# The second MLP's second product by Strassen's algorithm, with its weight forms built during attention

## The chip, the cores and the metric

The kernel runs on one core of a Trainium2 chip. The metric is the device time of one execution in microseconds (us); three timed runs of the kernel before gave a median of 886.11 us.

## The reference

Attention with a block-causal mask (4 batches, 8 heads, 576 positions, head dimension 64), then two MLPs over the 2304 tokens of width 512:

```
scores = q @ k.T / 8, masked where block(i) < block(j) (blocks of 64); softmax; attn @ v
x  = heads side by side                                  # 2304 x 512
x  = max(x @ w1, x @ w2, x @ w3) @ w_out                 # first MLP, hidden width 768
h  = max(x @ w_in, 0)                                    # second MLP, hidden width 2048
out = (h * h) @ w_out                                    # 2304 x 512
```

Weights of the MLPs come in double precision, read as pairs of 32-bit words; everything else is float32.

## The kernel before

**Precision.** A product of two float32 matrices is made of three TensorE products in float32r: each operand is split into a high part (a copy that rounds) and a low part (the subtraction of that copy), and low x high, high x low and high x high are summed in PSUM. So each product costs three matmuls per 128 x 128 block of weights, and each operand costs one copy (mostly on ScalarE) and one subtraction (on VectorE). `load_w_` (line 381) turns a block of 128 x 512 double-precision weights into float32 with integer operations: two ScalarE instructions, two on VectorE, one integer addition on GpSimd.

**Order of work.** All instructions go through a planner (`Plan`, line 187 issues them; so nearly every row of the profile has line 187). It knows an estimated length and a rank for each, and places them by a list schedule: on each engine the one that can start first, and among those the lowest rank, then program order. The result is one fixed order per engine and one for the DMA queue on SyncE (SP). There are two such plans, ended by `nc.issue()`: the first has attention, the first MLP up to its fifth of eight parts, and the preparation of w_out; the second has the rest of the first MLP, the preparation of w_in, and the second MLP. `nc.behind(marks[WO][0])` (line 781) holds back the preparation of w_out until the exponential of a certain attention step has been made; steps are counted in program order (20 steps for the first batch, 20 for each later one).

**Attention and first MLP.** Four batches, four head pairs each; `mlp1(b, g)` works on 256 or 320 tokens of a batch with the weights stationary. Its matmuls (tile `l` in the profile) fill TensorE beside attention, and what is left of them runs alone before the second MLP. Its output y goes to DRAM transposed (features by tokens).

**Second MLP, first product (up).** Three passes over 768 tokens each. In a pass the tokens form two halves of 384 columns, and features and hidden rows are cut in two as well, so that Strassen's algorithm (in Winograd's form) takes seven products p1 to p7 in place of eight. Its weight forms (a11, a12, a22 and four sums s1 to s4) are made once per block q (of eight): `second_rows` and `first_rows` (lines 806 and 810) load two row blocks, sum them on GpSimd and split them into `wq` [128, 7, 2, 256], which goes to DRAM as one piece of 1.79 MB and comes back in one piece per block and pass. Four blocks fit in the chip at a time, and the first pass uses the last four as they are made. `up(p, q)` (line 894) makes the seven products, 6 matmuls of 384 columns for each, with two PSUM banks X and Y; `part` and `finish` combine them on VectorE and ScalarE, apply relu and square, and split the result g.

**Second MLP, second product (down).** `down(p, q)` (line 946) is the plain product: for the four quarters of a block (two row blocks, two token halves) and three groups of 128 tokens, g is stationary and w_out moving, 3 matmuls of 512 columns each: 36 per block, summed over all eight blocks of a pass in six PSUM banks `acc`. It runs one block behind `up` and interleaved with it. w_out was split into high and low parts during late attention (tile `wos`, rows of `wo_d`); each block loads them again in pieces of 256 KB (tiles `wol`, `woh`). The output is tokens by features.

Of the kernel before, what the change touches and what calls it, by code (L numbers as in the profile page):

```python
# [44 lines left out]
CFG = dict(PD=-1, PE=1, A1=0, A2=0, WP=1, FC=(8, 16), WO=55, FI=0, LO2=0, HI2=0, Q2=0, RN=3, XL=2, HL=2, SO=0, TF=0, W_A=0.7, W_B=1.5, SPARE='hl..rhl..rhl..r..r..r', S=15, PB=3, QB=(2, 2, 3), BANKS=(3, 2, 1, 2), LO=0, HI=0, Q=0, EV=('*', '*'), EV2=('a', 'a'), CB=2, PC=0, PM=1000, PX=-0.5, PO=0, HH='*', XH='*', N0='a', YS='a', HIS=0, RB=1, TB=(2, 1), KB=1, CT='a', LT='d', XA=4, XB=0)  # L45
# [302 lines left out]
def fused_kernel(ctx: ExitStack, tc: tile.TileContext, z0, k0, qk, v, w123, wo1, win2, wo2, out):  # L348
# [15 lines left out]
    wo_d = dram.tile([NC2, 128, 2, DM], F32, name="wo_d")  # L364
    wq_d = dram.tile([NQ, 128, 7, 2, 256], F32, name="wq_d")
# [15 lines left out]
    def load_w_(src, hi, lo, name, f=None):  # L381
        spare = SPARE[len(chunks)] if len(chunks) < len(SPARE) else "."
        chunks.append(name)
        if spare in "hl":
# [9 lines left out]
        nc.sync.dma_start(out=raw, in_=src.bitcast(U32).rearrange("p (n t) -> p n t", t=2))  # L394
# [15 lines left out]
        if hi is None:  # L410
            return
# [26 lines left out]
    def load_wo1(c):  # L438
        wo1_t[c] = [m1.tile([128, DM], F32R, tag=f"wo1{x}{c}", name=f"wo1{x}{c}") for x in "hl"]
        load_w(wo1[128 * c:128 * c + 128, :], *wo1_t[c], f"wo1_{c}")  # L440
# [70 lines left out]
    def new_x(b, g):  # L511
        if (b, g) not in x_t:
            w = GROUPS[g][1]
            x_t[b, g] = [m1.tile([128, KC, w], F32R, tag=f"{t}{g}", name=f"{t}{b}_{g}") for t in ("xh", "xl")]
        return x_t[b, g]
# [264 lines left out]

    with nc.behind(marks[CFG["WO"]][0]), nc.ranked(2):
# [17 lines left out]
    wq_t, forms_f = {}, {}  # L799
    WB = 4  # L800

    def wq_tile(q):
        wq_t[q] = w2p.tile([128, 7, 2, 256], F32R, tag="wq", bufs=WB, name=f"wq{q}")
        return wq_t[q]

    def second_rows(q):
        f = forms_f[q] = w2p.tile([128, 8, 256], F32, tag="wqf", name=f"wqf{q}")
        load_w_(win2[q + NQ], None, None, f"wi_{q + NQ}", f[:, 0:2].rearrange("p i n -> p (i n)"))

    def first_rows(q):  # L810
        f, w = forms_f[q], wq_tile(q)
        load_w_(win2[q], None, None, f"wi_{q}", f[:, 2:4].rearrange("p i n -> p (i n)"))
        a21, a22, a11, a12, s1, s2, s3, s4 = [f[:, i] for i in range(8)]
# [3 lines left out]
        for i, j in ((0, 3), (3, 7)):  # L817
            nc.scalar.copy(out=w[:, i:j, 0], in_=f[:, i + 1:j + 1])
            nc.vector.tensor_tensor(out=w[:, i:j, 1], in0=f[:, i + 1:j + 1], in1=w[:, i:j, 0].bitcast(F32), op=ALU.subtract)
        nc.sync.dma_start(out=wq_d[q], in_=w.bitcast(F32))  # L820
# [16 lines left out]
    PRODUCTS = dict(p1=(1, "b11"), p2=(2, "b21"), p6=(4, "t2"), p5=(3, "t1"), p7=(5, "t3"), p3=(6, "b22"), p4=(0, "t4"))  # L837
# [27 lines left out]
    wo_t, g_t = {}, {}  # L865
    G_HOMES = [(m1, "xh0"), (m1, "xl0"), (m1, "xh1"), (m1, "xl1"), (m1, "hh"), (m1, "hl"), (w1p, "w1l5")]
    C_HOMES = ["wo1h4", "wo1l4", "wo1h5", "wo1l5"]
    homes = [0, 0]

    def wo_tiles(p, m):  # L870
        i = 2 * (m % NQ % 2) + m // NQ
        wo_t[p, m] = [m1.tile([128, DM], F32R, tag=f"wo1{c}{i}", name=f"wo{c}{p}_{m}") for c in "hl"]
        return wo_t[p, m]

    def load_wo(p, m):
        for c, t in enumerate(wo_tiles(p, m)):
            nc.sync.dma_start(out=t.bitcast(F32), in_=wo_d[m, :, c])

    def g_tiles(name):
        pool, tag = G_HOMES[homes[0] % len(G_HOMES)]  # L880
        homes[0] += 1
        g = pool.tile([128, 2, TH], F32R, tag=tag, name=name)
        return g[:, 0], g[:, 1]

    def split_g(key, c):
        gh, gl = g_t[key] = g_tiles("g%d_%d_%d_%d" % key)
        nc.scalar.copy(out=gh, in_=c)
        nc.vector.tensor_tensor(out=gl, in0=c, in1=gh.bitcast(F32), op=ALU.subtract)

    def c_tile(name):  # L890
        homes[1] += 1
        return m1.tile([128, TH], F32, tag=C_HOMES[homes[1] % len(C_HOMES)], name=name)

    def up(p, q):

        w, x = wq_t[q], x_s[p]
        X, Y = [bank(f"ph{p}_{q}_{b}", "mlp")[:, :TH] for b in "xy"]

        def product(acc, name):
            i, form = PRODUCTS[name]  # L900
            hi, lo = x[form]
            for k in range(2):
                ws = slice(128 * k, 128 * k + 128)
                for c, (s, r) in enumerate(((1, hi), (0, lo), (0, hi))):
                    mm(acc, w[:, i, s, ws], r[:, k], start=k == 0 and c == 0, stop=k == 1 and c == 2)
            if q == NQ - 1 and p + 1 < NPASS:
                split_tokens(p + 1, form)

        def part(acc, name, other=None):
            t = m1.tile([128, TH], F32, tag="xf", bufs=4, name=f"{name}_{p}_{q}")  # L910
            if other is None:
                nc.scalar.copy(out=t, in_=acc)
            else:
                nc.vector.tensor_tensor(out=t, in0=acc, in1=other, op=ALU.add)
            return t

        def finish(m, h, acc, other):
            c = c_tile(f"c{p}_{q}_{m}{h}")
            nc.vector.tensor_tensor(out=c, in0=acc, in1=other, op=ALU.add)
            nc.vector.scalar_tensor_tensor(out=c, in0=c, scalar=0.0, in1=c, op0=ALU.max, op1=ALU.mult)  # L920
            split_g((p, q, m, h), c)

        product(X, "p1")
        p1 = part(X, "p1")
        product(Y, "p2")
        finish(0, 0, Y, p1)
        yield 3
        product(X, "p6")
        u2 = part(X, "u2", p1)
        product(Y, "p5")  # L930
        u4 = part(Y, "u4", u2)
        yield 2
        product(X, "p7")
        finish(1, 1, X, u4)
        u3 = part(X, "u3", u2)
        yield 2
        product(Y, "p3")
        finish(0, 1, Y, u4)
# [43 lines left out]
    with nc.ranked(1):  # L982
        before = iter(())
        stream = [(p, q) for p in range(NPASS) for q in range(NQ)]
        for j, (p, q) in enumerate(stream):
# [13 lines left out]
            for _ in before:  # L999
                pass  # L1000
# [48 lines left out]
```

## Time and profile before

| | us |
|---|---|
| timed runs, median (lowest to highest) of 3 | 886.11 (885.11 to 886.7) |
| the profiled execution, span from first to last instruction | 886.9 |
| TensorE busy in it | 864.2 |
| VectorE, ScalarE, GpSimd busy | 601.1, 424.9, 104.0 |
| first matmul of the second MLP starts at | 501.71 |
| last matmul of all starts at | 881.76 |

The span is that of one execution with the profiler on; the timed runs are others. Busy time of TensorE is modelled from the starts of its matmuls and their lengths, and the matmuls overlap; the pace of a stretch is read from the starts, not from the busy time of one.

### The profile page before, as it was taken

The page shows a single profiled execution, that of the slowest core. Times are in us where ns is not written, and L with a number is a line of the kernel's source. Part 1 is how long each engine was busy: PE and PEld are TensorE (multiplying, and loading weights), DVE is VectorE, ACT ScalarE, POOL GpSimd, SP SyncE. Part 2 cuts the span into 40 slices and gives each one's busy share as a digit, 9 for nine tenths or more (in the row PEclk, how much of TensorE's full clock was granted, in tenths as well). Part 3 has the DMA queues.
Part 4 walks back from the last instruction along what each step waited for, and adds up shares of the span by engine and source line. Part 5 has one row for each costly group of instructions (what it writes and reads, how often), then busy time and mean ns, then how long its engine had stood idle before and what let it go on. Part 6 is the DMA issues. An engine that isn't in the chain of part 4 may idle for free.

```text
span 886.9 us, 14852 instructions
## 1 busy us (share of the span) xinstructions
PE 864.2 (97%) x5464; PEld 777.7 (88%) x5464; DVE 601.1 (68%) x1376; ACT 424.9 (48%) x1016; POOL 104.0 (12%) x94
## 2 busy tenths in 40 slices
PE   5899999999999999999999989999999999999997
PEld 4567799998999989899999979898999989999896
DVE  6998678878788988646557766546755457544543
ACT  6888667667688787544555231113211114211111
POOL 2233200000001111214442230000000000000000
PEclk9999999999999999999999999999999999999999
DMA  8745432232255563554656578454765536655221
GB/s 294 237 138 174 131 114 89 85 115 86 85 184 177 175 213 118 196 190 165 257 203 237 164 299 338 160 230 168 270 229 184 207 145 229 215 200 196 72 72 71
DMA packets 52056, 157.73 MB, mean 178 GB/s; under 512 B 8592, under 2 KB 16016, under 8 KB 48400
## 3 DMA queue, kind: packets, MB, share of 16 engines
q1 hardware_dynamic: 51984, 156.78, 50.5%
q8 instruction: 43, 0.70, 0.3%
q14 instruction: 29, 0.24, 0.1%
HBM read 124.26 MB, written 32.51 MB: 177 GB/s over the span
## 4 chain that ended last, share of the span: by engine, by line
PE 92%; DVE 2%; DMA 2%; ACT 2%; issue 0%; POOL 0%; SPq 0%; ACTq 0%; POOLq 0%; DVEq 0%
PE l L187 34%; PE acc L187 22%; PE ph_x L187 11%; PE ph_y L187 8%; PE av L187 5%; PE sc L187 5%; PE tp L187 4%; PE sc_t L187 2%; DMA raw_wi<-in_win 1%; PE tp_t L187 1%; DMA raw_wo<-in_wo 1%; DMA zk<-in_k 1%; PE r L187 0%; ACT P L187 0%; DVE f_wo L187 0%
## 5 line engine op out<-in xcount | busy, mean ns | idle before, releaser
L187 PE MATMUL acc<-woh,g 128*128 128x512 f32 x576 | 198.5, 395 | 0.0
L187 PE MATMUL l<-xh,w1l 128*128 128x256 f32 (+1 forms) x576 | 174.3, 303 | 0.9 <-DVE run L187 0.9
L187 PE MATMUL l<-xl,w1h 128*128 128x256 f32 (+1 forms) x576 | 172.2, 299 | 0.0
L187 PE MATMUL l<-xh,w1h 128*128 128x256 f32 (+1 forms) x576 | 172.2, 299 | 0.0
L187 ACT CAST g<-c 128x384 fp32r<-128x384 f32 x96 | 49.3, 513 | 220.8 <-DVE c L187 220.8
L187 PEld LDWEIGHTS acc<-woh,g 128*128 128x128 f32 x576 | 108.5, 189 | 19.4
L187 PE MATMUL acc<-wol,g 128*128 128x512 f32 x288 | 113.3, 393 | 0.0
L187 PEld LDWEIGHTS l<-xh,w1l 128*128 128x128 f32 x576 | 109.0, 189 | 4.1 <-issue 1.5
L187 PEld LDWEIGHTS l<-xl,w1h 128*128 128x128 f32 x576 | 109.1, 189 | 2.6 <-issue 1.7
L187 PEld LDWEIGHTS l<-xh,w1h 128*128 128x128 f32 x576 | 109.1, 189 | 1.9 <-issue 1.2
L187 PE MATMUL ph_x<-t,wq 128*128 128x384 f32 x432 | 87.7, 337 | 2.7 <-ACT p L187 2.7
L187 PEld LDWEIGHTS ph_x<-t,wq 128*128 128x128 f32 x432 | 77.4, 188 | 8.9 <-ACT p L187 3.1
L187 DVE TENSOR_TENSOR g<-c,g 128x384 fp32r<-128x384 f32 x96 | 53.6, 560 | 43.0 <-ACT g L187 42.6
L187 ACT ACTIVATE P<-sc,nm 128x128 f32<-128x128 f32 (+3 forms) x128 | 66.9, 530 | 9.9 <-DVE nm L187 8.4
L187 DVE TENSOR_TENSOR run<-l,run 128x256 f32<-128x256 f32 (+1 forms) x96 | 43.7, 455 | 27.9 <-PE l L187 26.3
L187 POOL TENSOR_TENSOR f_wo<-f_wo,raw_wo 128x512 int32<-128x512 int32 x22 | 29.8, 1357 | 276.5 <-DVE sm L187 180.3
L187 PEld LDWEIGHTS acc<-wol,g 128*128 128x128 f32 x288 | 54.3, 189 | 7.8
L187 PE MATMUL l<-hh,wo1l 128*128 128x256 f32 (+1 forms) x192 | 57.7, 306 | 2.2 <-DVE wo1l L187 2.1
L187 PE MATMUL ph_y<-b,wq 128*128 128x384 f32 x288 | 58.3, 337 | 0.0
L187 PE MATMUL l<-hl,wo1h 128*128 128x256 f32 (+1 forms) x192 | 57.5, 301 | 0.0
L187 PE MATMUL l<-hh,wo1h 128*128 128x256 f32 (+1 forms) x192 | 57.4, 300 | 0.0
L187 DVE TENSOR_REDUCE nm<-sc 128x2 f32<-128x256 f32 (+2 forms) x96 | 55.1, 588 | 0.8
(135 smaller groups left out, 1613.1 us busy)
## 6 DMA issues: line engine op xcount, KB each, us to landing
wq<-wq_d SPq DMA_DIRECT2D x20, 1792.0 KB, 8.6
wq_d<-wq SPq DMA_DIRECT2D x8, 1792.0 KB, 7.7
raw<-in_qk SPq DMA_DIRECT2D x24, 576.0 KB, 3.8
wol<-wo_d SPq DMA_DIRECT2D x48, 256.0 KB, 3.2
woh<-wo_d SPq DMA_DIRECT2D x48, 256.0 KB, 4.8
raw_wo<-in_wo SPq DMA_DIRECT2D x22, 512.0 KB, 3.8
raw_w<-in_w SPq DMA_DIRECT2D x18, 512.0 KB, 5.0
wo_d<-wos SPq DMA_DIRECT2D x16, 512.0 KB, 3.1
```

The source lines that it names most:

```text
L187: return getattr(engine, op_name)(*map(value, args), **{k: value(x) for k, x in kw.items()})
```

## The change

The second product of the second MLP goes through the same seven products as the first. For that:

- the output is made transposed (features by tokens), w_out's forms are stationary and g is moving, 384 columns at a time; the program returns the transpose of what it wrote;
- `down_forms(q)` builds the seven forms of each of eight blocks of w_out (sums on GpSimd, one copy and one subtraction for each form of 256 columns) and stores each with a DMA of 256 KB. It starts at attention step 24 in place of 55;
- `up_forms(q)` builds the forms of w_in with rank 0.5 in place of 2, all eight blocks in order, with the raw rows loaded one block ahead, and stores all of them to DRAM;
- both products now work on pairs of blocks j (four per pass). A unit of weights is one form of one pair (512 KB, two DMAs); 56 units per pass pass through a ring of nine tiles, in which the raw rows and the staged forms of w_in had their place before;
- in both products partial sums stay in PSUM: p1 is copied out and p6 is added on top of it in the same bank, and so on. Four banks per pair in up, six per pass in down;
- a pass is now four up pairs, then all of down; sums and splits of g are made in place ahead of the products that need them.

```diff
-CFG = dict(..., WO=55, ...)
+CFG = dict(..., WO=24, ...)
...
+    def split_form(pool, tag, bufs, f, dest, name):
+        n = f.area.shape[1] // 256
+        both = pool.tile([128, n, 2, 256], F32R, tag=tag, bufs=bufs, name=name)
+        f = f.rearrange("p (i n) -> p i n", n=256)
+        nc.scalar.copy(out=both[:, :, 0], in_=f)
+        nc.vector.tensor_tensor(out=both[:, :, 1], in0=f, in1=both[:, :, 0].bitcast(F32), op=ALU.subtract)
+        nc.sync.dma_start(out=dest.rearrange("i p h n -> p i h n"), in_=both.bitcast(F32))
+    def down_forms(q):
+        f = [load_w_(wo2[128 * m:128 * m + 128, :], None, None, f"wo_{m}") for m in (q, q + NQ)]
+        a11, a21, a12, a22 = [x[:, 256 * i:256 * i + 256] for x in f for i in range(2)]
...
+        combine(s1, a21, a22, ALU.add)
+        split(a11, "a11")
+        combine(a21, a11, a21, ALU.subtract)
+        split(a22, "a22")
...
     with nc.behind(marks[CFG["WO"]][0]), nc.ranked(2):
-        for m in (m for q in range(NQ) for m in (q, q + NQ)):
-            t = at.tile([128, 2, DM], F32R, tag="wos", name=f"wos{m}")
-            load_w_(wo2[128 * m:128 * m + 128, :], t[:, 0], t[:, 1], f"wo_{m}")
-            nc.sync.dma_start(out=wo_d[m], in_=t.bitcast(F32))
+        for q in range(NQ):
+            down_forms(q)
...
+    def up_forms(q):
+        fa, fs = [w2p.tile([128, 4, 256], F32, tag="gq", bufs=5, name=f"w{x}{q}") for x in ("fa", "fs")]
+        if q == 0:
+            load_raw(0)
+        if q + 1 < NQ:
+            load_raw(q + 1)
...
+        for f, i, j in ((fa[:, 1:2], 0, 1), (fa[:, 2:4], 1, 3), (fs[:, 0:2], 3, 5), (fs[:, 2:4], 5, 7)):
+            split_form(w2p, "ws", RING, f.rearrange("p i n -> p (i n)"), ws_d[0][q][i:j], f"wst{q}_{i}")
-    with nc.ranked(2):
-        for q in (*range(WB, NQ), *range(WB)):
-            second_rows(q)
-            first_rows(q)
+    with nc.ranked(0.5):
+        for q in range(NQ):
+            up_forms(q)
...
+    UP = ("p1", "p2", "p6", "p5", "p7", "p3", "p4")
+    DOWN = ("p1", "p5", "p6", "p3", "p7", "p2", "p4")
...
+    for p in range(NPASS):
+        stream += [(0, j, WEIGHT[i]) for j in range(NPQ) for i in UP]
+        stream += [(1, j, WEIGHT[i]) for i in DOWN for j in range(NPQ)]
...
+            u = w2p.tile([128, 2, 2, 256], F32R, tag="ws", bufs=RING, name=f"ws{len(units)}")
+            for a in range(2):
+                nc.sync.dma_start(out=u[:, a].bitcast(F32), in_=ws_d[s][2 * j + a][FORMS[form]])
...
+    BANKS_UP = ((("mlp", "mlp"), ("tp", "tp")), (("sc", "sc"), ("sc", "av")))
+    BANKS_DOWN = ((("mlp", "mlp"), ("tp", "tp"), ("sc", "sc")), (("sc", "sc"), ("sc", "av"), ("tp", "tp")))
+    def up(p, j):
+        X, Y = banks(BANKS_UP[(p + j) % 2], f"ph{p}_{j}")
+        acc = dict(p1=X, p6=X, p7=X, p4=X, p2=Y, p5=Y, p3=Y)
...
+        for name in UP:
+            w = next_unit()
+            hi, lo = x_s[p][TOKENS[name]]
+            for a in range(2):
+                o = acc[name][a]
+                for k in range(2):
+                    ws = slice(128 * k, 128 * k + 128)
+                    for c, (s, r) in enumerate(((1, hi), (0, lo), (0, hi))):
+                        mm(o, w[:, a, s, ws], r[:, k], start=name in ("p1", "p2", "p5") and k == 0 and c == 0, ...)
+                if name in ("p1", "p6", "p5"):
+                    nc.scalar.copy(out=keep[name, a], in_=o)
...
+    def ahead(p, j):
+        first_g[p, j] = split_g(p, "p1", j, g_c[j, "b11"])
+        sum_g(j, "t1")
+        sum_g(j, "t3")
+    def down(p):
+        X, Z, Y = banks(BANKS_DOWN[p % 2], f"acc{p}")
+        acc = dict(p1=X, p6=X, p7=X, p4=X, p5=Z, p3=Z, p2=Y)
+        for name in DOWN:
+            for j in range(NPQ):
+                if name == "p1":
+                    hi, lo = first_g.pop((p, j))
+                else:
+                    if form in ("t2", "t4"):
+                        sum_g(j, form)
+                    hi, lo = split_g(p, name, j, g_c[j, HELD[form]])
+                w = next_unit()
+                for a in range(2):
+                    for n in range(2):
+                        ns = slice(128 * n, 128 * n + 128)
+                        for c, (s, r) in enumerate(((1, hi), (0, lo), (0, hi))):
+                            mm(acc[name][n], w[:, a, s, ns], r[:, a], ...)
...
+                up(p, j)
+                ahead(p, j)
+            down(p)
```

## Rows read from the trace of the kernel before

**Rows 1.** The page: span, and busy us (share) xinstructions of TensorE and VectorE.
```profile
span 886.9 us, 14852 instructions
...
PE 864.2 (97%) x5464; PEld 777.7 (88%) x5464; DVE 601.1 (68%) x1376; ACT 424.9 (48%) x1016; POOL 104.0 (12%) x94
```

**Rows 2.** Windows of 20 us: length, busy (count) by engine, PEclk, DMA share, GB/s.
```profile
260.00:280.00 20.00, 20.00 (x148) 17.94 (x147) 17.86 (x52) 17.84 (x48) 2.62 (x2) 1.00 0.49 169
...
500.00:520.00 20.00, 17.30 (x94) 15.88 (x93) 13.33 (x24) 8.28 (x15) 6.52 (x7) 1.00 0.91 338
520.00:540.00 20.00, 20.00 (x95) 18.15 (x94) 13.83 (x24) 4.79 (x9) 5.94 (x6) 0.91 0.71 264
```

**Rows 3.** TensorE's timeline at the second MLP's start: start, length, [idle before].
```profile
501.71 1.20 PE L187 MATMUL ph_x<-b,wq 128*128 128x384 f32 x6
...
506.93 0.39 PE L187 MATMUL acc<-woh,g 128*128 128x512 f32 x1
...
516.42 0.40 PE L187 MATMUL acc<-woh,g 128*128 128x512 f32 x1
519.52 1.50 PE L187 MATMUL ph_x<-t,wq 128*128 128x384 f32 x6 [2.70 <-ACT p L187]
...
524.67 0.39 PE L187 MATMUL acc<-woh,g 128*128 128x512 f32 x1
```

**Rows 4.** The chain of waits in order of time: start, length, what (xcount).
```profile
369.51 132.36 PE l L187 x972
...
507.94 10.06 DMA raw_wi<-in_win
...
688.06 2.08 PE acc L187 x9
...
735.08 2.08 PE acc L187 x9
```

**Rows 5.** ScalarE's timeline at the stall of 516 us.
```profile
516.67 0.65 ACT L187 ACTIVATE raw_wi<-raw_wi 128x512 int32<-128x512 uint32 x1 [4.05 <-DMA raw_wi<-in_win]
...
519.00 0.47 ACT L187 COPY p<-ph_x 128x384 f32<-128x384 f32 x1
```

**Rows 6.** Groups by form: operation, shapes, count, busy us, mean ns, idle before.
```profile
L187 DVE SCALAR_TENSOR_TENSOR c<-c 128x384 f32<-128x384 f32 x96 | 53.6, 560 | 2.0
...
L187 POOL TENSOR_TENSOR wqf<-wqf 128x256 f32<-128x256 f32 x32 | 26.9, 862 | 1.2
...
L187 DVE TENSOR_TENSOR wos<-f_wo,wos 128x512 fp32r<-128x512 f32 x16 | 12.1, 754 | 11.6 <-ACT wos L187 10.9 <-ACT run L187 0.6
...
L187 DVE TENSOR_TENSOR t<-t,t 128x768 fp32r<-128x768 f32 x12 | 11.3, 952 | 2.0 <-ACT t L187 2.0
L187 DVE TENSOR_TENSOR hl<-run,hh 128x256 fp32r<-128x256 f32 x24 | 11.1, 464 | 1.8 <-ACT hh L187 1.4
...
L187 ACT CAST wos<-f_wo 128x512 fp32r<-128x512 f32 x16 | 9.9, 620 | 10.7 <-DMA wo_d<-wos 10.7
...
L187 ACT CAST hh<-run 128x256 fp32r<-128x256 f32 x16 | 6.5, 406 | 8.3 <-DVE run L187 8.0
```

**Rows 7.** A window of 1 us within output-weight loads, columns as in rows 2.
```profile
825.00:826.00 1.00, 1.00 (x6) 0.83 (x5) 0.96 (x2) 0.00 (x0) 0.00 (x0) 1.00 0.99 336
```

**Rows 8.** DMA issues: count, KB each, median us from issue to landing.
```profile
wol<-wo_d SPq DMA_DIRECT2D x48, 256.0 KB, 3.2
```

**Rows 9.** Waits of SP's queue: us in total, times, longest.
```profile
SPq L187 <- DVE wos L187: 23.4, 9, 6.9
```

**Rows 10.** The tile wos: ns min/median/max, first and last start.
```profile
L187 DVE TENSOR_TENSOR wos<-f_wo,wos x16: 664/689/1851, 272.6 to 392.0; 128x512 fp32r<-128x512 f32 x16
```

**Rows 11.** Timelines at the end: TensorE's last row, VectorE's last row.
```profile
881.76 0.39 PE L187 MATMUL acc<-woh,g 128*128 128x512 f32 x1
...
882.59 1.05 DVE L187 COPY ob<-acc 128x256 f32<-128x256 f32 x2 [2.43 <-ACT ob L187]
```

More of the change, by code (lines that the diff above doesn't have):

```diff
@@ L393, in load_w_ @@
                 f = m1.tile([128, 512], F32, tag="wf", bufs=2, name=f"f_{name}")
-        nc.sync.dma_start(out=raw, in_=src.bitcast(U32).rearrange("p (n t) -> p n t", t=2))
+        if src is not None:
+            nc.sync.dma_start(out=raw, in_=src.bitcast(U32).rearrange("p (n t) -> p n t", t=2))
         low, high = raw[:, :, 0], raw[:, :, 1]
@@ L438, in load_wo1 @@
     def load_wo1(c):
-        wo1_t[c] = [m1.tile([128, DM], F32R, tag=f"wo1{x}{c}", name=f"wo1{x}{c}") for x in "hl"]
+        if not wo1_t:
+            both = m1.tile([128, NC1, 2, DM], F32R, tag="wo1", name="wo1")
+            wo1_t.update({i: [both[:, i, x] for x in range(2)] for i in range(NC1)})
         load_w(wo1[128 * c:128 * c + 128, :], *wo1_t[c], f"wo1_{c}")
@@ L513, in new_x @@
             w = GROUPS[g][1]
-            x_t[b, g] = [m1.tile([128, KC, w], F32R, tag=f"{t}{g}", name=f"{t}{b}_{g}") for t in ("xh", "xl")]
+            both = m1.tile([128, 2, KC, w], F32R, tag=f"xhl{g}", name=f"xhl{b}_{g}")
+            x_t[b, g] = [both[:, i] for i in range(2)]
         return x_t[b, g]
@@ L894, in up @@
[L894 to L910, printed above, removed]
+    NPQ = NQ // 2
@@ new lines, in next_unit, with make_homes @@
+    def next_unit():
+        while len(units) < used[0] + RING:
+            n = len(units)
+            load_unit()
+            if len(units) == n:
+                break
+        used[0] += 1
+        return units[used[0] - 1]
+    C_HOMES = [("xhl1", 3), ("hh", 2), ("hl", 2), ("wo1", 8), ("xhl0", 1)]
+    g_c = {}
+    def make_homes():
+        places = []
+        for tag, n in C_HOMES:
+            t = m1.tile([128, n, 2, TH], F32, tag=tag, name=f"c_{tag}")
+            places += [t[:, i] for i in range(n)]
+        for j in range(NPQ):
+            for f in ("b11", "b12", "b22", "b21"):
+                g_c[j, f] = places.pop(0)
@@ new lines, in fused_kernel, with split_g, temp @@
+    turn_g = [0]
+    def split_g(p, name, j, f):
+        home = turn_g[0] % 6
+        turn_g[0] += 1
+        both = (w2p.tile([128, 2, 2, TH], F32R, tag="gq", bufs=5, name=f"g{p}_{name}_{j}") if home else
+                w1p.tile([128, 2, 2, TH], F32R, tag="w1l5", name=f"g{p}_{name}_{j}"))
+        nc.scalar.copy(out=both[:, 0], in_=f)
+        nc.vector.tensor_tensor(out=both[:, 1], in0=f, in1=both[:, 0].bitcast(F32), op=ALU.subtract)
+        return both[:, 0], both[:, 1]
+    def temp(tag, bufs, name):
+        return m1.tile([128, TH], F32, tag=tag, bufs=bufs, name=name)
@@ new lines, in fused_kernel, with banks, finish @@
+    BANKS_UP = ((("mlp", "mlp"), ("tp", "tp")), (("sc", "sc"), ("sc", "av")))
+    BANKS_DOWN = ((("mlp", "mlp"), ("tp", "tp"), ("sc", "sc")), (("sc", "sc"), ("sc", "av"), ("tp", "tp")))
+    def banks(tags, name):
+        return [[bank(f"{name}_{x}{i}", t)[:, :TH] for i, t in enumerate(pair)] for x, pair in zip("xzy", tags)]
+    def up(p, j):
+        X, Y = banks(BANKS_UP[(p + j) % 2], f"ph{p}_{j}")
+        acc = dict(p1=X, p6=X, p7=X, p4=X, p2=Y, p5=Y, p3=Y)
+        keep = {}
+        def finish(a, form, f, other):
+            c = g_c[j, form][:, a]
@@ L911, in part @@
             if other is None:
-                nc.scalar.copy(out=t, in_=acc)
+                nc.scalar.copy(out=c, in_=f)
             else:
[L914 to L919, printed above, removed]
-            nc.vector.scalar_tensor_tensor(out=c, in0=c, scalar=0.0, in1=c, op0=ALU.max, op1=ALU.mult)
-            split_g((p, q, m, h), c)
@@ L923, in up @@
[L923 to L938, printed above, removed]
-        yield 2
-        product(X, "p4")
-        finish(1, 0, X, u3)
-        yield 3
```

193 lines of the change are left out of this document (96 added, 97 removed).

## The prediction

> **What bounds the kernel now.** I read the page first: TensorE is busy 97% of a span of 886.9 us, VectorE 68% [rows 1]. A busy share of 97% can hide slow stretches, so I went to the second MLP, the stage that the change rewrites. Windows of 20 us show its two edges: TensorE is full with the granted clock at 1.00 on either side, and in 500:520 and 520:540 it loses time and the clock falls to 0.91 [rows 2]. The timeline gives the price of one matmul there, from start to start. The stage starts at 501.71; its first five up products (30 matmuls of 384 columns, nothing between them) take until 506.93, so 5.22/30 = 0.174 us each [rows 3]. The chain of waits repeats a pattern, one block of FF rows (42 up, 36 down matmuls) per period; three periods lie between 688.06 and 735.08, so 15.673 us each [rows 4]. Up takes 42 x 0.174 = 7.31 of it, and 8.37/36 = 0.232 us is left for a down matmul of 512 columns. The chain in this stretch names TensorE alone: no wait ends last there. So work taken off TensorE in this stage comes off the end, one for one, until another engine or the DMA is late.
>
> The one stall of the stage is at its start. TensorE's next matmul after 516.42 starts at 519.52, 2.70 us idle, released by ScalarE's copy p [rows 3]. That copy starts at 519.00, behind a weight conversion for which ScalarE had sat idle 4.05 us until a DMA of raw w_in rows landed [rows 5]; the chain shows that DMA as the piece of 10.06 us from 507.94 on [rows 4]. The 18 matmuls from 519.52 to 524.67 then run at about half the pace, at the lower of the clock's two levels in part (0.91 over the 20 us) [rows 2, 3]: 5.15 us for 12 x 0.174 + 6 x 0.232 = 3.48. Idle and slow clock together cost 2.9 + 1.7 = 4.6 us (the matmul at 516.42 would have ended its turn at 516.65).
>
> **The change part by part.** *The second product.* Before: 24 blocks x 36 = 864 matmuls of 512 columns, 864 x 0.232 = 200.8 us. After: 3 passes x 7 products x 4 pairs x 12 = 1008 matmuls of 384 columns. The trace has this shape with the same three terms (low weight, low data, high both) in the up product: 1008 x 0.174 = 175.4 us. Bounds: a down matmul now costs 0.232 - 0.2133 = 0.019 us over its columns at 2.4 GHz, an up matmul 0.014; were the 0.019 a property of this place and not of the shape, the new one takes 0.179 and the product 180.5. I take 0.174, the row of the same shape. Gain 25.4 us (20.3 at the other end). The up product keeps 1008 matmuls of 384 columns: nothing.
>
> *The stall.* The forms of w_in are moved ahead in rank (from 2 to 0.5, in front of the first MLP's matmuls but behind its evictions), their raw rows are loaded one block ahead, and nothing holds two whole blocks back any more. Before, the chain from 369.51 on is 132.36 us of unbroken matmuls (972) with the forms beside them [rows 4]; GpSimd is the longest in a block's forms (4 x 0.862 us for the sums [rows 6], and two integer additions), so eight blocks fit in that stretch twice over. I count 3.6 of the 4.6 us as won and leave 1.0 for what is late next: the first units' loads, whose ring slots are those that the last forms were staged in. Bounds: 0 to 4.6.
>
> *Evictions and splits of the stage.* Up, per pair of blocks: 6 additions and 8 relu-squares on VectorE at 0.56 and 3 instructions of 768 columns at 0.95 [rows 6], 10.7 us beside 84 x 0.174 = 14.6 us of TensorE; ScalarE has fewer. In the last pair of a pass the seven token splits come on top (7 x 0.95): 17.3 us against 14.6. The 2.7 us over spill into the down products, because the banks there are other ones and the first splits were made earlier. Down, per pass: 24 splits and 8 sums of 0.95 make 30 us beside 58.5. A product's partial sum is copied out while the other pair of banks gets the next product (12 matmuls, 2.09 us, against a copy and a queue of about 0.56 + 0.95 us); that wait is new, and behind it in TensorE's queue stands everything. I cost it at nothing; if VectorE were one split later than planned at each of the 36 up evictions that precede a reuse, it would be some 0.3 us each, 10 us.
>
> *Weights from DRAM.* Before, 1.79 MB per block, of which the last four blocks stayed in the chip for the first pass, and the output weights in 256 KB loads. Now each unit of 12 matmuls needs two loads of 256 KB, rows of 2 KB, every 2.09 us: 0.524/2.09 = 251 GB/s, with tokens and outputs (9.4 MB over 351 us) 278 GB/s. The same rows of 2 KB, in the output-weight loads before, moved 336 GB/s in a microsecond in which the DMA engines were busy 0.99 [rows 7]; so the stream needs some 0.83 of them. One such load lands 3.2 us after issue [rows 8]; the ring of nine units gives eight units, 16.7 us, of lead. SP's issues, two per unit, pass in well under 1 us. Cost zero, with an upper end below.
>
> The Trainium skill, "DMA: Bandwidth & Descriptors", section "Bandwidth", speaks against this: batch DMAs to at least 1 MiB for 75% of peak, with 1 MB at 341 GB/s and 64 KB at 138 GB/s. An estimate from that page, between those two for 256 KB, is some 240 GB/s, which is under the need, and by it the stage would end some 15% later than TensorE alone would. The row of 336 GB/s has several 256 KB loads in flight and does not agree with it as a limit on a stream.
>
> *Forms of w_out, during attention.* Before, 16 rows each with one copy (0.620) and one subtraction (0.754). After, 56 forms of 256 columns, for which the nearest rows are 0.406 and 0.464 [rows 6]: ScalarE 22.7 - 9.9 = +12.8 us, VectorE 26.0 - 12.1 = +13.9 us, GpSimd 32 x 0.862 = +27.6 us, and 56 stores in place of 16. The start moves from mark 55 to mark 24, so it is spread over the attention of three batches and not of one and a half. What covers it is the first MLP's matmuls: in 260:280 the old forms were begun, VectorE stood at 17.86 of 20 us, and TensorE was at 20.00 at full clock [rows 2]. The denser load after the move is no denser than that, so I cost it at 0. Cover gone: all 13.9 us of VectorE plus a few stalls. On SP's queue a store waits for its subtraction, and behind it wait attention's loads; before, such waits were 23.4 us in 9 cases, 2.6 each [rows 9].
>
> Of the 16 old subtractions one took 1.851 us where the median is 0.689 [rows 10]; GpSimd's additions run beside them. The Trainium skill, "SBUF — State Buffer", section "Who interferes with whom", says that GpSimd and a VectorE instruction with two SBUF inputs exclude each other on a shared port for a whole instruction. By it the 27.6 us of GpSimd sums could lengthen VectorE's two-input work by as much, to about 41 us more in attention. VectorE has some 2 us in 20 free in the fullest windows and more before them, so the sum stays.
>
> *The end.* The last matmul starts at 881.76; then two eviction pieces on VectorE that end at 883.64 [rows 11] and the store. After: one addition or copy of 384 columns on each of two engines, 0.56 us after the last matmul, instead of about 1.5: -0.9 us.
>
> **Sum**, on the profiled execution (span 886.9): -25.4 - 3.6 - 0.9 = -29.9, 857.0. The span lies 0.8 us above the median of the three timed runs (886.11) and 0.2 above their highest; nothing else of that execution's time is given, so I set the timed run at span minus 0.8: 856.2, rounded up to 857 for the small things on the new path.
>
> **The rivals.** *A, the stall comes back or a new one takes its place* (ring slots not free, a form late): 857 + 3.6 plus up to 4.6 more, 861 to 865. For it: ScalarE still waits in order behind a DMA. Against: the raw rows come a block ahead. *B, attention pays*: VectorE's 13.9 us and up to 27.6 us of blocked port are partly on the path, 862 to 880. For it: VectorE at 17.86 of 20 us. Against: TensorE was full in that same window. *C, the ring runs dry, the slower side*: the stream is the bound in the second MLP. A unit that takes u us instead of 2.09 adds 168 x (u - 2.09). It is slower than before from u = 2.27 on, which is 231 GB/s of weights; at 220 GB/s it is 2.38 us, +49 us, 906. Between 251 and 231 GB/s it eats part of the gain, 858 to 886. For it: the longest stretch at a high rate is 338 GB/s in 20 us at 0.91 busy [rows 2], in large pieces; no window holds 278 for 350 us. Against: 336 GB/s with the same rows of 2 KB. The Trainium skill's rule on 1 MiB, cited above, would make this rival true. *D, it does not do what it says*: the down matmul keeps its 0.019 us and evictions stall TensorE, 862 to 872.
>
> **How the numbers follow.** Forecast as summed 0.60 (853 to 861). A 0.10, B 0.12, D 0.08. C 0.10, of which half slower than before. The range is 852 to 872: it holds the forecast, A, D and most of B, and leaves out C's larger half and B's end, some 0.12. Below 852 nothing but attention getting shorter would lead, and TensorE is full there. About 0.2% (1.8 us) is what a measurement here can tell from no change: faster 0.93, same 0.02, slower 0.05.
>
> **What would show it.** Right: a pass of 117 us (4 x 14.6 + 58.5) between the first up matmuls of two passes; clock 1.00 in 500:540; the start of the second MLP within 3 us of 501.7; DMA busy near 0.8. Wrong: TensorE idle on a DMA of the weight units (C), on ScalarE or VectorE copies in up (D), the second MLP starting after 505 (B or A).

## The result, and the profile after

Timed runs of the changed kernel have a median of 860.46 us (858.69 to 860.54, 4 runs), those of the kernel before 886.4 (885.11 to 888.75, 4 runs): a ratio of 0.9705 with a 95% interval of 0.968 to 0.9729. The prediction was 857.0 in a range of 852 to 872. The profiled execution went from a span of 886.9 us to 858.4, 28.5 less, and these can be placed by the first and the last matmul of the second MLP: it starts at 502.04 and was at 501.71 (+0.3); it lasts to 854.98, 352.9 us, and took 380.4 (-27.5); what follows the last matmul takes 3.4 and took 4.75 (-1.3).

The page of the kernel after, and windows of it (length, busy and count for PE, PEld, DVE, ACT and POOL, PEclk, DMA share, GB/s), beside [rows 1, 2]:

```profile
span 858.4 us, 15996 instructions
...
PE 836.4 (97%) x5608; PEld 786.6 (92%) x5608; DVE 641.3 (75%) x1389; ACT 486.1 (57%) x1138; POOL 131.0 (15%) x126
```

```profile
120.00:360.00 240.00, 238.93 (x1812) 217.12 (x1811) 210.05 (x621) 185.48 (x526) 39.45 (x40) 1.00 0.53 171
...
500.00:520.00 20.00, 17.12 (x100) 16.79 (x100) 10.95 (x18) 4.59 (x10) 0.00 (x0) 1.00 1.01 366
520.00:540.00 20.00, 20.00 (x117) 20.00 (x117) 14.12 (x25) 6.11 (x13) 0.00 (x0) 1.00 1.01 364
600.00:840.00 240.00, 240.00 (x1386) 240.00 (x1385) 158.55 (x230) 89.04 (x144) 0.00 (x0) 1.00 0.83 267
```

The same window of attention in the kernel before:

```profile
120.00:360.00 240.00, 240.00 (x1822) 218.19 (x1820) 197.50 (x593) 179.63 (x498) 14.05 (x11) 1.00 0.42 135
```

The reader is to see three things. From 600 on TensorE is full, at full clock, with the DMA engines at 0.83. 500:520 still has a hole of some 3 us, and the hole has changed its cause: GpSimd does nothing there now (6.52 us before), while the DMA is full, in 520:540 as well. And in 120:360, where attention carries the new forms, GpSimd has 39.45 us instead of 14.05, VectorE 210.05 instead of 197.50, and TensorE has lost 1 us.

TensorE's timeline of the kernel after, at the start of the second MLP, at the start of its second pass and at the fourth pair of its third (start, length, form, count, idle before):

```profile
502.04 2.30 PE L187 MATMUL ph_x<-b,ws 128*128 128x384 f32 x12
504.18 2.26 PE L187 MATMUL ph_z<-b,ws 128*128 128x384 f32 x12
...
510.46 2.26 PE L187 MATMUL ph_x<-t,ws 128*128 128x384 f32 x12
515.60 2.31 PE L187 MATMUL ph_z<-b,ws 128*128 128x384 f32 x12 [2.88 <-DMA ws<-ws_d]
517.75 2.24 PE L187 MATMUL ph_x<-t,ws 128*128 128x384 f32 x12
...
621.79 2.24 PE L187 MATMUL ph_x<-b,ws 128*128 128x384 f32 x12
...
781.99 2.24 PE L187 MATMUL ph_x<-b,ws 128*128 128x384 f32 x12
...
846.50 8.48 PE L187 MATMUL acc_x<-g_p,ws 128*128 128x384 f32 x48
```

From 621.79 to 781.99 are 77 units of 12 matmuls, a whole pass (56) and three pairs of the next one's up (21): 2.0805 us per unit, 0.1734 per matmul, in up and down alike. A pass is so 56 x 2.0805 = 116.5 us. The first pass took 621.79 - 502.04 = 119.75, which is 3.25 more. Of these, 3.06 are the one wait of TensorE in the whole stage: 5.14 us from the unit at 510.46 to the next, where a unit takes 2.08. The chain of waits (start, length, what) shows what stands behind it, and the pace of down:

```profile
374.81 127.39 PE l L187 x932
506.93 8.53 DMA ws<-ws_d
...
596.98 8.33 PE acc_x L187 x48
605.30 8.32 PE acc_y L187 x48
```

So the -27.5 are these: before, the two products at their pace took 24 x 15.673 = 376.2 us [rows 4]; after, 3 x 116.5 = 349.5; that is -26.7. What lies over the pace was 380.4 - 376.2 = 4.2 and is 3.4: the stall was not removed, it gave back 0.8.

**Why the stall stayed.** The load that TensorE waits for was issued at 506.93, into a ring slot in which the last forms of w_in had been staged. GpSimd's timeline of the kernel after, in the eighth and last block of these forms:

```profile
474.06 1.31 POOL L187 TENSOR_TENSOR wfa<-wfa,raw_wi 128x512 int32<-128x512 int32 x1 [5.27 <-issue]
475.45 0.74 POOL L187 TENSOR_TENSOR wfs<-wfa 128x256 f32<-128x256 f32 x1
492.90 1.31 POOL L187 TENSOR_TENSOR wfa<-wfa,raw_wi 128x512 int32<-128x512 int32 x1 [16.72 <-ACT t L187]
```

The seven blocks before it went through at some 12 us each; this one stood still for 16.7 us in its middle. What ScalarE and VectorE did in that time, beside the first MLP's evictions (`run`, `hh`, `hl`), are the token sums and splits of the first pass (tiles `t` and `b`): their rank is 0 and that of the forms 0.5, so wherever both could go, the tokens went. VectorE's timeline at the end of the gap: the forms' instruction comes at 492.09, behind the tokens, and GpSimd's addition follows it.

```profile
490.65 0.95 DVE L187 TENSOR_TENSOR t<-yf,t 128x768 f32<-128x768 f32 x1
491.68 0.49 DVE L187 TENSOR_TENSOR run<-l,run 128x320 f32<-128x320 f32 x1
492.09 0.69 DVE L187 SCALAR_TENSOR_TENSOR wfa<-raw_wi,wfa 128x512 int32<-128x512 int32 x1
```

The last forms were stored from 498.6 to 506, around the start of the second MLP at 502.04.

### The profile page after: what moved, and what is told of

The parts are those of the page before. It is cut to its first block, busy times and chain, and to the rows that moved or that the text cites. A ratio compares the mean times of both kernels' runs of the same rounds, so it can differ in the third digit from the quotient of the medians.

```text
span 858.4 us, 15996 instructions
## 1 busy us (share of the span) xinstructions
PE 836.4 (97%) x5608; PEld 786.6 (92%) x5608; DVE 641.3 (75%) x1389; ACT 486.1 (57%) x1138; POOL 131.0 (15%) x126
## 4 chain that ended last, share of the span: by engine, by line
PE 93%; DMA 3%; ACT 2%; DVE 2%; SPq 0%; issue 0%; ACTq 0%; DVEq 0%
PE l L187 35%; PE acc_x L187 12%; PE ph_x L187 11%; PE ph_z L187 8%; PE acc_z L187 6%; PE av L187 6%; PE sc L187 5%; PE tp L187 4%; PE acc_y L187 3%; PE sc_t L187 2%; DMA ws<-ws_d 1%; PE tp_t L187 1%; DMA raw<-in_qk 1%; DMA ws_d<-wst 1%; DMA zk<-in_k 1%; ACT P L187 0%
## 5 line engine op out<-in xcount | busy, mean ns | idle before, releaser
L187 PE MATMUL l<-xhl,w1h 128*128 128x320 f32 (+1 forms) x1152 | 244.8, 300 | 0.0
L187 PEld LDWEIGHTS l<-xhl,w1h 128*128 128x128 f32 x1152 | 188.4, 190 | 4.5 <-issue 2.9
L187 PE MATMUL l<-xhl,w1l 128*128 128x256 f32 (+1 forms) x576 | 175.0, 304 | 0.0
L187 PEld LDWEIGHTS l<-xhl,w1l 128*128 128x128 f32 x576 | 109.3, 190 | 3.4 <-issue 1.5
L187 PE MATMUL acc_x<-g_p,ws 128*128 128x384 f32 x576 | 102.2, 335 | 0.0
L187 PEld LDWEIGHTS acc_x<-g_p,ws 128*128 128x128 f32 x576 | 100.1, 188 | 0.0
L187 PE MATMUL l<-hh,wo 128*128 128x320 f32 (+1 forms) x384 | 81.6, 298 | 2.9 <-DVE wo L187 2.1
L187 PE MATMUL ph_x<-t,ws 128*128 128x384 f32 x432 | 80.8, 335 | 0.0
L187 PEld LDWEIGHTS ph_x<-t,ws 128*128 128x128 f32 x432 | 75.4, 188 | 0.0
L187 PEld LDWEIGHTS l<-hh,wo 128*128 128x128 f32 x384 | 63.3, 190 | 3.7 <-DVE wo L187 2.5
```

Source lines behind the costliest of these rows:

```text
L187: return getattr(engine, op_name)(*map(value, args), **{k: value(x) for k, x in kw.items()})
```

## Experiments

**1. The forms ahead of the tokens.** If this is the cause, letting the first pass's token work come after the forms takes the stall away.

```diff
-    with nc.ranked(0):
+    with nc.ranked(0.7):
         load_tokens(0)
```

> The first pass's token sums and splits get rank 0.7 in place of 0, behind the forms of w_in (0.5). Theory: the 2.9 us stall of TensorE at 512.7 comes from the last block of w_in's forms, which waits from 475 to 492 us behind the token splits on VectorE and ScalarE and so keeps four ring slots until after 500. Then the block ends near 482, the ring is full before the second MLP starts, the stall goes, and the span falls by 2.5 to 3 us (858.4 to about 855.5). Rival 1 (the DMA engines are simply full when the second MLP starts): the stall stays within 1 us of 2.9 and the time is the same. Rival 2 (the tokens are then what is late): a wait of TensorE on token splits near 502 us of 2 us or more, time the same or up to 3 us longer.

Measured: 853.44 (852.69 to 854.82), ratio to the kernel before 0.9637 [0.9609, 0.9664], against 0.9705 for the change alone: the best version. GpSimd's timeline of this kernel in its last block:

```profile
471.80 0.74 POOL L187 TENSOR_TENSOR wfs<-wfa 128x256 f32<-128x256 f32 x1
473.41 1.31 POOL L187 TENSOR_TENSOR wfa<-wfa,raw_wi 128x512 int32<-128x512 int32 x1 [0.88 <-ACT hh L187]
```

and its windows:

```profile
480.00:500.00 20.00, 20.00 (x137) 20.00 (x136) 12.99 (x19) 6.55 (x11) 0.00 (x0) 1.00 0.98 341
500.00:520.00 20.00, 20.00 (x117) 20.00 (x116) 15.13 (x26) 7.39 (x16) 0.00 (x0) 1.00 0.86 272
```

The 16.7 us in the middle of the block are 0.9, the loads of the weight units begin some 20 us earlier (DMA share 0.98 in 480:500), and TensorE waits for nothing in the second MLP. Its first pass runs from the first to the second of these rows:

```profile
498.39 2.24 PE L187 MATMUL ph_x<-b,ws 128*128 128x384 f32 x12
...
614.90 2.24 PE L187 MATMUL ph_x<-b,ws 128*128 128x384 f32 x12
```

That is 116.5 us, the pace of a pass, and 3.2 less than in the kernel after, of the 7.0 between the medians. The edit moves the token loads in SP's queue too, so it shows that the order was the cause, but not which queue's. Another 3.65 us of difference are in the start of the second MLP (498.39 against 502.04), and they are in place before 371 us, while the edit lies in the second plan: the chains of the two executions are 1.4 us apart at the first MLP's matmuls around 51 us, 2.5 behind a load of q and k around 105 us, and 3.6 from 223 us on. So this part differs from execution to execution and is not put down to the edit: the stage starts at 502.04 and 500.76 in the two executions of the kernel after, and at 498.39 to 500.21 in the four with the edit. Over all runs here the four sets with this edit (three of them stand below) have medians of 853.4 to 856.9, mean 854.9, the three sets without it 859.6 to 860.9, mean 860.3. The difference is 5.4 us, where the stall cost 3.1, 4.4 and 5.2 us in the three executions without the edit (the kernel after, experiments 2 and 6).

**2. The change once more**, as a control in a later set of runs, no edit.

> The changed kernel as it is, once more, to see how large the loss at the start of the second MLP is in another execution, since putting the tokens behind the forms gained 7.0 us in the medians and the profile of the changed kernel shows only 2.9 us of idle there. Theory (the idle varies with how early the first MLP ends, as in the one-load version, which ended it 3 us sooner and then lost 3.3 us of idle and 1.7 of slow clock): idle and slow clock together 3 to 6 us, median 859 to 861. Rival (2.9 us is all, and the two runs differed by their first 120 us): median 856 to 858.

860.85 (856.91 to 862.25, 6 runs), ratio 0.9706 [0.9681, 0.9731]. The same wait is there, at the same instruction, with 2.58 us idle. Rows of TensorE's timeline, and the window (columns as above):

```profile
500.76 2.31 PE L187 MATMUL ph_x<-b,ws 128*128 128x384 f32 x12
...
509.27 2.28 PE L187 MATMUL ph_x<-t,ws 128*128 128x384 f32 x12
514.13 3.88 PE L187 MATMUL ph_z<-b,ws 128*128 128x384 f32 x12 [2.58 <-DMA ws<-ws_d]
517.85 2.28 PE L187 MATMUL ph_x<-t,ws 128*128 128x384 f32 x12
...
622.82 2.24 PE L187 MATMUL ph_x<-b,ws 128*128 128x384 f32 x12
```

```profile
500.00:520.00 20.00, 17.42 (x92) 17.10 (x91) 9.71 (x16) 4.52 (x9) 0.00 (x0) 0.91 1.03 369
```

Here the granted clock was 0.91 over the 20 us, at the lower of its two levels for a part of them behind the wait, and the unit there took 3.72 us in place of 2.08. The first pass took 622.82 - 500.76 = 122.06, 5.6 over its pace. Of these, 2.8 are the wait (4.86 us from unit to unit at 509.27) and 1.6 the slow unit: the stall cost 4.4. The other 1.1 are not the stall: from the start of the stage, before the wait, until some 564 us a unit took 2.12 us in place of 2.08, at a granted clock shown as 1.00, and no run here shows why. In the first execution the clock had stayed at 1.00 after 2.88 us idle, and the stall cost the 3.1 of the wait.

**3. The two halves of the change that met at the stall, each alone in the kernel before.** The new rank of w_in's forms, and the new start of w_out's forms:

```diff
-    with nc.ranked(2):
+    with nc.ranked(0.5):
         for q in (*range(WB, NQ), *range(WB)):
```

> The kernel before with one edit: w_in's forms get rank 0.5 in place of 2. Theory (the stall of 4.6 us at 516 us in the kernel before is a form that comes late, and a higher rank alone does not cure it, since the first pass's token splits at rank 0 stay ahead and one staging buffer holds one block at a time): the last forms still end after 500 us and the time changes by -3 to +1 us. Rival (the rank is what removes the stall): -4 to -5 us.

```diff
-WO=55
+WO=24
```

> The kernel before with one edit: the preparation of w_out starts at attention step 24 in place of 55. Theory (beside attention the forms are covered by the first MLP's matmuls, wherever they are put): attention's last exponential moves by less than 3 us and the time by less than 3 us either way, most likely 1 to 2 us faster since w_in's forms can begin sooner after attention. Rival (the early start costs attention): 3 to 8 us slower.

The rank alone gave 888.42 (12 runs), ratio 1.003 [1.0009, 1.0051]: slightly slower. The start alone gave 883.04 (12 runs), ratio 0.9962 [0.9943, 0.998]. Windows of 500:520, the rank first, then the start:

```profile
500.00:520.00 20.00, 15.97 (x86) 14.25 (x86) 15.48 (x22) 8.18 (x14) 12.01 (x11) 1.00 1.00 364
```

```profile
500.00:520.00 20.00, 19.83 (x103) 17.94 (x102) 17.34 (x29) 6.56 (x12) 6.31 (x6) 1.00 0.79 293
```

With the rank alone the forms still run to 519 (GpSimd 12.01 us in this window) and the hole is larger. With the early start alone it closes: w_out's forms end at 303 us, not at 392 [rows 10], and the second MLP starts at 498.68. So moving the start cost attention nothing in the old kernel and gained about 3 us.

**4. w_out's forms late, as before.** The prediction gave their early start no worth of its own and said what a lost cover would cost: 13.9 us of VectorE plus a few stalls.

```diff
-WO=24
+WO=55
```

> The preparation of w_out starts at attention step 55 again (about 265 us) in place of 24 (about 134 us); all else as in the changed kernel. Theory (the early start is what makes room: a block of w_out's forms takes some 31 us beside attention, eight blocks fill 134 to 383): only three or four blocks are ready when attention ends near 365, the rest take some 6 to 8 us each, w_in's forms start near 400 to 410 in place of 386 and end 15 to 25 us later, so the second MLP's ring is late and TensorE stalls for 5 to 20 us at its start. Rival (the start doesn't matter, low rank finds room anyway): within 2 us of the changed kernel. Rival (the early start costs attention): 2 to 6 us faster than the changed kernel.

901.57 (900.62 to 902.95), ratio 1.0176 [1.0147, 1.0205]: 41 us over the kernel after, slower than the kernel before. The stall that was expected at the start of the second MLP is there (10.4 us), but three times as much stands in a place that was not expected. The waits of TensorE (engine, tile, released by: us in total, times, longest) and a window:

```profile
PE l L187 <- ACT run L187: 29.7, 1, 29.7
PE ph_x L187 <- DMA ws<-ws_d: 10.4, 1, 10.4
```

```profile
400.00:420.00 20.00, 0.00 (x0) 0.00 (x0) 11.38 (x20) 7.92 (x17) 9.34 (x9) 0.50 0.58 197
```

TensorE stands still for 20 us with VectorE at 57% and ScalarE at 40%: no engine is the bound, an order is. ScalarE's timeline of this kernel:

```profile
422.44 0.40 ACT L187 CAST wst<-f_wo 128x256 fp32r<-128x256 f32 x1 [1.72 <-DMA ws_d<-wst]
423.30 0.40 ACT L187 CAST wst<-f_wo 128x256 fp32r<-128x256 f32 x1 [0.45 <-DVE wst L187]
424.12 0.40 ACT L187 CAST wst<-f_wo 128x256 fp32r<-128x256 f32 x1 [0.42 <-DMA ws_d<-wst]
424.43 0.42 ACT L187 COPY run<-l 128x320 f32<-128x320 f32 x1
```

The forms are at the end of the first plan. Their chain (copy, subtraction, store, three staging tiles) takes some 12 us a block when nothing lies between, and the first MLP's evictions (`run`), which are in the second plan, stand behind all of it in ScalarE's queue. When the last copy is through, at 424.12, the eviction follows at once.

**5. w_out's forms twice.** Each form split and stored a second time, at the early start: does attention pay for VectorE's work?

```diff
-        split_form(at, "wst", 3, x, ws_d[1][q][i:i + 1], ...)
+        for s in (1, 2):
+            split_form(at, "wst", 3, x, ws_d[s][q][i:i + 1], ...)
```

> In the changed kernel, every form of w_out is split and stored twice (the second time to a place that nothing reads): 56 more ScalarE copies, 56 more VectorE subtractions and 56 more stores of 256 KB during attention. Theory (the forms are hidden beside attention, but only until the first plan's matmuls run out near 380 us; behind that point the forms hold ScalarE's queue and TensorE stands still, as with the late start of step 55): blocks take 40 us and more in place of 31, five or six are done when attention ends, attention's own end moves by another 5 to 15 us, and TensorE then idles once for 10 to 30 us: +12 to 35 us. Rival (VectorE and ScalarE have room for them): within 3 us of 860. Rival (the split work lies on the path all along): attention 25 us longer and +23 us or more with TensorE's idle time spread over it.

911.85 (909.73 to 913.64), ratio 1.0287 [1.0254, 1.0319], 51 us over the kernel after where 12 to 35 were expected, and not in the way expected. Attention did not end later. ScalarE's copies of its output (last start) in the kernel before, in the kernel after and here:

```profile
L187 ACT COPY xf<-av x24: 372/400/432, 119.6 to 363.0; 128x256 f32<-128x256 f32 x12, 128x320 f32<-128x320 f32 x12
```

```profile
L187 ACT COPY xf<-av x24: 356/387/428, 120.1 to 374.9; 128x256 f32<-128x256 f32 x12, 128x320 f32<-128x320 f32 x12
```

```profile
L187 ACT COPY xf<-av x24: 352/401/430, 118.2 to 363.5; 128x256 f32<-128x256 f32 x12, 128x320 f32<-128x320 f32 x12
```

The waits of TensorE:

```profile
PE l L187 <- ACT run L187: 40.9, 1, 40.9
PE ph_x L187 <- DMA ws<-ws_d: 12.0, 1, 12.0
```

It is the wait of experiment 4: the forms ran to 432.9 us, and the evictions stood behind them. Attention yields nothing; what does not fit beside it is left at its end, and there it costs its whole chain.

**6. One load of 512 KB in place of two of 256 KB per unit**, rows of 4 KB in place of 2: is the size of the piece a limit of the stream?

```diff
-            for a in range(2):
-                nc.sync.dma_start(out=u[:, a].bitcast(F32), in_=ws_d[s][2 * j + a][FORMS[form]])
+            nc.sync.dma_start(out=u.bitcast(F32), in_=ws_d[s][j][FORMS[form]])
... (the stores put the two halves side by side)
```

> A weight unit is stored so that its two halves lie together in DRAM: one load of 512 KB with rows of 4 KB in place of two of 256 KB with rows of 2 KB. The bytes are the same. Theory (TensorE is the bound in the second MLP, the stream has room): the pace from unit to unit stays 2.083 us, the time changes only through the stall at the start, at most -2 to 0 us; the DMA busy share in 620:800 falls a little from 0.82 if a row costs anything of its own. Rival (size of a load matters, as the rule on 1 MiB says): DMA busy share falls by more than 0.1 and the stall of 2.9 us goes, -3 us.

859.61 (858.46 to 862.47), ratio 0.9706 [0.968, 0.9733]: the same. DMA share in 600:800 is 0.83 at 268 GB/s, as with the two loads. The stall did not go with the larger load; it stands at the first unit:

```profile
502.74 3.06 PE L187 MATMUL ph_x<-b,ws 128*128 128x384 f32 x12 [3.34 <-DMA ws<-ws_d]
```

The first two units took 2.86 and 2.97 us, at a granted clock of 0.91 over 500:520; with the wait the stall cost 5.2 us.

**7. More bytes than the units need**, to find where the stream runs dry: a copy of 256 KB from DRAM to DRAM beside each unit's loads.

```diff
+                nc.sync.dma_start(out=spare_d[len(units) - 1], in_=ws_d[s][2 * j][FORMS[form]])
```

> Each unit issues a third transfer of 256 KB, a copy from DRAM to DRAM that nothing reads: 1.5 times the bytes of the stream, 377 GB/s needed with TensorE at full pace, 404 with tokens and outputs. Theory (the DMA engines carry at most the 365 GB/s that 500:540 showed at a busy share of 1.01): the stream is the bound, 141.6 MB at 365 GB/s make 388 us for the second MLP in place of 353, so about +35 us, with TensorE waiting on weight loads throughout. Rival (365 was not a limit, for the loads had all been issued by then): +0 to 10 us.

949.17 (946.5 to 951.51), ratio 1.0711 [1.0677, 1.0745]: 89 us over the kernel after where 35 were expected, and it says nothing of the limit. Nothing held the copies in their place, so they were issued between 402 and 596 us and stood ahead of other transfers on SP's queue (TensorE waited 63.5 us once, for ScalarE's `ys`). When they were gone, the pace was 2.095 us per unit up to some 636 us and 2.08 again from 735 on.

Two kernels then held each copy behind the last matmul of the unit whose ring slot the load beside it takes, from the 30th load on, one with a copy for every second unit and one with a copy for each; both on top of experiment 1, so that no stall lies in them. A third had copies with rows of 2 KB.

```diff
+            n = len(units) - 1 - RING
+            if n >= 20:          # the first of them: and n % 2
+                with nc.behind(ends[n]):
+                    nc.sync.dma_start(out=spare_d[n], in_=ws_d[s][2 * j][FORMS[form]])
... (`ends[n]` is set at each matmul of unit n; the rank of experiment 1)
```

> On the version with the tokens behind the forms (853.4 us, no stall in the second MLP): from the 30th unit on, every second unit issues one more transfer of 256 KB in the same queue, a copy from DRAM to DRAM that nothing reads, held in order behind the last matmul of the unit whose ring slot it follows. 1.25 times the bytes: 315 GB/s of stream, some 340 with tokens and outputs. Theory (the engines carry 365 GB/s, so the change left a margin of about a quarter): TensorE stays at 2.083 us per unit, +0 to 2 us, DMA busy share near 1.0. Rival (the margin is smaller than the busy share of 0.82 says): a wait on weight loads in most units, +15 to 40 us.

> As paced_x125, but one such copy for every unit: 377 GB/s of stream, some 404 in all. Theory (365 GB/s is the limit): the stream becomes the bound from the 30th unit on, 138 units at 0.786 MB plus 7 MB of tokens and outputs at 365 GB/s take 317 us in place of 288, so +25 to 35 us, TensorE waiting on weight loads and the DMA busy share at 1.0. Rival (copies between DRAM addresses are cheaper or the limit is higher): +0 to 10 us.

> As the 1.5-fold stream before (854.8 us, no wait on a load), but the extra copies write rows of 2 KB with gaps between them, so that they are made of 128 rows of 2 KB like the weight loads, and not of 16 rows of 16 KB. Theory (rows of 2 KB cost what rows of 16 KB cost, per byte): no wait of TensorE on weight loads, within 2 us of 854.8. Rival (it was the long rows that left room; rows of 2 KB end near the 365 GB/s of 500:540): TensorE waits on weight loads from about the 40th unit on, +25 to 40 us.

856.9, 854.75 and 854.69 us; ratios 0.966 [0.9624, 0.9695], 0.9642 [0.96, 0.9683], 0.9647 [0.9621, 0.9674]. TensorE waits for no load in the second MLP in any of them, and a pass takes 116.5 us. The first is 3.5 us over experiment 1 with fewer bytes than the second, so the 3.5 us are not put down to the bytes; its stage starts at 500.21 where that of experiment 1 starts at 498.39. A window of the first and one of the second:

```profile
650.00:800.00 150.00, 150.00 (x867) 150.00 (x867) 105.81 (x156) 58.13 (x96) 0.00 (x0) 1.00 0.95 327
```

```profile
650.00:800.00 150.00, 150.00 (x867) 150.00 (x867) 104.95 (x155) 58.94 (x98) 0.00 (x0) 1.00 1.03 389
```

The theory that 365 GB/s at a share of 1.01 (the window 500:540 of the kernel after) was the limit falls: with half as many bytes again per unit the engines carry 389 GB/s over 150 us at unchanged pace. Of these, 126 are the copies between DRAM addresses, counted once; the kernel after has 263 in the same window. Without such copies 397 GB/s went with a share of 1.01 in 500:520 of experiment 6. A load lands after 5.2 us there, 3.9 in the kernel after; the ring's lead of 16.7 us covers both. How much more it would carry was not tried.

## Why the prediction came out as it did

The mechanism of the main term was right, that of the stall was not, and the time was 3.5 us too low. The sum was 857.0 for the span, which is 858.4; that it came so near is in part luck, since 1.7 us more gained in the second product and at the end made up for part of the 2.8 that the stall did not give.

- **Pace of the second product: right, slightly under.** 0.174 us per matmul from the same shape in up [rows 3]; measured 0.1734. A pass was to take 117 us and takes 116.5. Gain 26.7 against 25.4, the difference being the 0.6 ns that 2016 matmuls multiply. Of the 26.7, 23.0 are columns (864 x 512 less 1008 x 384, at 2.4 GHz) and 3.7 time over the columns. The upper bound of 0.179 took the 0.019 us over the columns for a property of the place and not of the shape. It was indeed not of the shape: in the last down products of the kernel before, where no up product stands between them, 30 matmuls of 512 columns take 880.85 - 874.05 = 6.80 us, 0.2267 each and 0.013 over their columns. The 0.019 goes with the alternation of up and down, and the new order has whole runs of each in its place; so the bound was not needed, and rival D is out. TensorE's timeline of the kernel before at its end:

```profile
874.05 0.39 PE L187 MATMUL acc<-wol,g 128*128 128x512 f32 x1
...
880.85 0.39 PE L187 MATMUL acc<-wol,g 128*128 128x512 f32 x1
```

- **The stall: the step that failed.** "Eight blocks fit in that stretch twice over" counted GpSimd's work and left out who goes first on the other engines. 3.6 us were to be won and 1.0 left; 0.8 was won and 3.3 left (the stall cost 4.4 and 5.2 in two other executions). Rival A described it (ring slots not free, a form late) and had 0.10, and its lower end of 861 is about where the time came out. The order, not the work, was the cause: experiment 1 changes one rank and the wait is gone.
- **Evictions in PSUM banks at 0: right.** TensorE waits for no copy, sum or split in the second MLP.
- **Weights from DRAM at 0: right, with room.** A share of "some 0.83" was predicted and 0.83 measured, at 267 GB/s for 278. Rival C is out: half as many bytes again leave the pace as it is. The Trainium skill, "DMA: Bandwidth & Descriptors", section "Bandwidth" (batches of at least 1 MiB for 75% of peak, in a table of transfers issued from GpSimd), is not borne out as a rule on this stream of many transfers issued from SP: 256 KB and 512 KB pieces give the same time (experiment 6), and loads and copies of 256 KB reach 389 GB/s.
- **w_out's forms beside attention at 0: right where they stand; their price without cover far off.** VectorE's 56 subtractions took 24.7 us (48 at a mean of 0.439, eight at 0.508), where 0.464 each made 26.0; from 120 to 360 VectorE has 12.6 us more and the second MLP starts 0.3 us later. Attention itself does end 12 us later than before (374.9 against 363.0), but TensorE is full with the first MLP's matmuls meanwhile, so this is not on the path; and as it ends at 363.5 with the forms made twice, the forms are not shown to be its cause. The price was put at "13.9 us of VectorE plus a few stalls"; it is 41 us when the forms start late and 51 when they are doubled, because it is the chain through four queues that counts and not VectorE's share of it. Rival B had the wrong place: it looked at attention, and the cost lies at the seam behind it.
- **The shared port.** The Trainium skill, "SBUF — State Buffer", section "Who interferes with whom", would have allowed some 27 us of blocked VectorE, an estimate by its rule. GpSimd did 25.4 us more between 120 and 360, and VectorE's busy time rose by 12.6 us. The new subtractions there take 18.8 us where the old ones took 7.9, which is most of it; the instructions that both kernels have there took 2.7 us longer in all, by their means. The median subtraction is 0.418 us with single ones up to 0.954. So single instructions are stretched (no run here shows by whom), and the sum of it is small beside 27.
- **The end: right** (-1.3 for -0.9).
- **From span to timed run: wrong sign.** I took the timed run as span minus 0.8, since the span of 886.9 lay above the three times shown. In all other executions here the timed run is 1.7 to 2.1 above the span of the same execution, 2.1 in the kernel after. By that the span of 886.9 goes with the timed run of 888.75, the slowest of the four and not among the three shown. That is 2.1 of the 3.5 us; 1.4 are the sum.

Open: why the clock falls after a wait of 2.6 us in one execution and holds after 2.9 in another of the same kernel; why that first one has units of 2.12 us for its first 60 us of the stage; and whether more staging tiles for the forms would soften the cost of experiments 4 and 5, which was not tried.

## What to carry to other kernels

A preparation that "fits twice over" beside a stretch must be counted on every engine of its chain, with the ranks of whatever competes there: the engine with the most work (GpSimd) was not the one that was late. Where two in-order plans meet, ask what the first leaves at its end, since the second plan's evictions stand behind all of it; cost that at the chain's latency per item, not at an engine's busy time. And to ask whether a stream has room, add bytes that are held in step with it, or they will all run at once and measure a queue instead.

## What the runs showed of the hardware

A DMA busy share of 1.00 is not the limit of what the engines carry: 364 GB/s at 1.01 in 520:540 of the kernel after, 397 at 1.01 in 500:520 of experiment 6, 389 at 1.03 over 150 us with the extra copies (DRAM to DRAM, counted once).

In a stream of matmuls with a weight load for each, the time over the columns at 2.4 GHz is the same at three widths: 0.1734 - 0.160 = 0.013 us at 384 columns, 0.2267 - 0.2133 = 0.013 at 512 in the run of 30 down matmuls at the end of the kernel before, and 0.1467 - 0.1333 = 0.013 at 320 in the first MLP of the kernel after (27 matmuls from 497.78 to 501.74). The mean of 0.019 at 512 is that of the stretch in which up and down alternate every few matmuls; no run here shows what in the alternation costs the rest.
